# Attention followed by a sticky mixture of experts: a new order of the vector engine's round, other places for the operand splits and for the routing steps

## The chip, the cores and the metric

The kernel runs on one core of a Trainium2 chip. The metric is the device time of one execution in microseconds (us), as the median of the runs shown. Engines are named as in the profile: PE multiplies matrices (PEld loads their stationary side), DVE is the vector engine, ACT the scalar engine, POOL the GpSimd engine, and SP issues most of the DMA transfers.

## The reference

Two stages follow each other. The attention keeps, for each query, the first 4 keys and a window of 128 keys. The experts' stage picks for each token the expert with the largest logit, or keeps the expert of the token before it when a local gate says so, which makes the choice a scan along the sequence.

```python
# attention: batch 4, 8 heads, 768 positions, 64 per head, float32
scores = scale * np.matmul(q, k.transpose(0, 1, 3, 2))
keep = is_sink | in_window
scores = np.where(keep, scores, -1000000000.0)
a = np.exp(scores - np.max(scores, axis=-1, keepdims=True))
a = a / (np.sum(a, axis=-1, keepdims=True) + 1e-09)
x = np.matmul(a, v)                       # then reshaped to (4, 768, 512)
# experts: 8 of them, 512 -> 1024 -> 512
for s in range(S):
    fresh_e = int(np.argmax(logits[b, s]))
    e = fresh_e if s == 0 or local_gate[b, s] < 0.5 or prev_e < 0 else prev_e
    prev_e = e
    p = softmax(logits[b, s])
    out[b, s] = p[e] * (np.maximum(x[b, s] @ w1[e], 0.0) @ w2[e])
```

## The kernel before, in words

**Blocks, groups and rounds.** The attention works on 8 groups (4 batches by 2 halves of the heads, 4 heads each). A group has 6 blocks of 128 queries, numbered 0 to 5, so there are 48 blocks. The loop `for n in range(nb + 3)` runs rounds: round n scores block n, turns the probabilities of block n-1, multiplies block n-2 by the values and finishes block n-3. Rounds 0 to 47 have scores, rounds 48 to 50 drain the pipeline. PE, DVE and ACT run in the order in which this loop writes their instructions (`tc.manual_schedule`); POOL and SP get their order from the framework's planner. Every engine runs its own queue in order.

**One round.** `score` (L513) makes the scores of two units of two heads each. `out` runs once per unit: a DVE instruction masks the scores and takes their minimum (L525, two per unit), and ACT takes the exponential and its sum (L527). `pack` (L532, DVE) copies the sinks' probabilities of block n-1, where that block is 2 or later; PE turns them (L553), ACT copies them (L559) and DVE subtracts (L563). `turn` (L542, PE) and `turned` (L549, ACT) turn the other probabilities. `apply` (L573, L578, PE) multiplies by the values, `collect` (L466, DVE) copies the result out of PSUM, `back` (L470, PE) turns it back and multiplies by the gate weights, and `finish` (L485, L489, DVE) scales by the inverse sums. `sums` (L476, DVE) adds 1e-9 to the sums of the exponentials and `invert` (L479) inverts them.

Before the change DVE's order in a round is: out of unit 0, pack, out of unit 1, sums, finish, the subtraction L563, invert, one or more routing steps, collect.

**The splits.** Queries and keys are split into a high and a low part for a more exact product. For the next group POOL does this in `qk_split`: four copies (L118) and four subtractions (L123). `HEADS` says in which unit of the present group they are written; POOL waits only for its data and may run ahead of that place. Two tiles take turns: `w_a` for even groups, `qk_b` for odd ones.

**The routing.** When the last block of a batch is finished, `routing` is started as a generator, and `step` runs one piece of it, up to the next `yield`. Its pieces are: logits and their maximum (L238, L241); the choice (L247 to L261) and the exponentials' argument (L266); a transposition on PE (L274) with two ACT copies (L276, L278); two half scans (L286); two half counts (L293) with a rank (L295, on POOL for the first two batches, else on DVE); a matmul that brings slots and one-hot rows back (L301); slots and gates (L305 to L315); and six indirect stores per batch from POOL's queue into the buffer `xs` (L318). The fourth batch is routed in two parts: its first three blocks at the end of the attention, its last three (the tail) during the first expert rows. One step is taken per round before round 38, two from 38 on, three from 47 on.

**The first expert weights.** During the last group, `first_load` and `first_split` bring the first expert's first matrix and split it (L396 on DVE and ACT by turns, L397 on POOL, the last one on DVE). After round 50, `early_prep` turns the first rows of the first expert (L360) and the experts' stage begins: `ffn1` (L946, L955) and `second` (L1004).

Of the kernel before, what the change touches and what calls it, by code (L numbers as in the profile page):

```python
# [19 lines left out]
P = 128  # L20
# [25 lines left out]
FSK, FAST0 = 4, 38  # L46
LOADS = {0: (2,), 3: (0,), 4: (3, 1), 6: (4,), 8: (5,)}
HEADS = (6, 7, 9, 10), (4, 6, 8, 9)
LATER = 5, 6, 7, 8
# [3 lines left out]
RAW = 7200  # L53
WX = P + 2 * NW
# [10 lines left out]
def kernel(ctx, tc, qkd, vn, vs, w1, w2, nw, c_misc, c_ident, c_idw, c_small,  # L65
# [51 lines left out]
    def copy(e, out, in_):  # L117
        (nc.scalar.copy if e == "act" else getattr(nc, e).tensor_copy)(out, in_)  # L118

    lows = {}  # L120
# [4 lines left out]
    def qk_split(gi, eng, ahead=True, qc=slice(0, S), kc=slice(0, KPAD)):  # L125
        def part(p, x, cs, eng):
            hi, lo = qk_t[gi % 2][p][2 * x:2 * x + 2]
            r = raw[(gi * NPR + p) % NR][:, x]
            copy(eng[0], hi[:, cs], r[:, cs])
            low(eng[1], lo[:, cs], r[:, cs], hi[:, cs])  # L130
# [33 lines left out]
    with tc.tile_pool(name="ps_w", bufs=1, space=PS) as ps_w:  # L164
        wt = ps_w.tile([P, 512], F32, name="wt")
        zb = zrow.bitcast(BF16)
        for _ in range(WARM):
            nc.tensor.matmul(wt, zb[:, 0:P], zb[:, 0:512], start=True, stop=True)

# [42 lines left out]
    fk_t = rt.tile([P, NBLK, 40], BF16, name="fk")  # L212
    nc.gpsimd.memset(fk_t, 0.0)
# [17 lines left out]
    def routing(b, i0, i1, sfx, ps, ptag, apart=False):  # L231
# [4 lines left out]
        lg = rt.tile([P, NBLK, NW], F32, tag="lg", name=f"lg{n}")  # L236
        lg = lg[:, 0:nb]
        nc.vector.tensor_reduce(out=lg, in_=lw[:, i0:i1].rearrange("p i h e -> p i e h"), axis=AX.X, op=ALU.add)  # L238
        mx = rt.tile([P, NBLK], F32, tag="mx", name=f"mx{n}")
        mx = mx[:, 0:nb]  # L240
        nc.vector.tensor_reduce(out=mx, in_=lg[:, :, 0:E], axis=AX.X, op=ALU.max)  # L241
        if apart:
            yield
        mxb = mx.unsqueeze(2).broadcast_to([P, nb, E])
        eq = rt.tile([P, NBLK, E], F32, tag="eq", name=f"eq{n}")
        eq = eq[:, 0:nb]
        nc.vector.tensor_tensor(out=eq, in0=lg[:, :, 0:E], in1=mxb, op=ALU.is_equal)  # L247
        nc.vector.tensor_tensor(out=eq, in0=eq, in1=rank_w[:, 0:nb], op=ALU.mult)
        m2 = rt.tile([P, NBLK], F32, tag="m2", name=f"m2{n}")
        m2 = m2[:, 0:nb]  # L250
        nc.vector.tensor_reduce(out=m2, in_=eq, axis=AX.X, op=ALU.max)
        fr = rt.tile([P, NBLK], F32, tag="fr", name=f"fr{n}")
        fr = fr[:, 0:nb]

        nc.vector.scalar_tensor_tensor(out=fr, in0=lg[:, :, E], scalar=-1.5 * 2.0 ** -23,
                                       in1=first[:, i0:i1], op0=ALU.is_lt, op1=ALU.max)
        fk = fk_t[:, 0:nb]
        nc.vector.tensor_tensor(out=eq, in0=eq, in1=m2.unsqueeze(2).broadcast_to([P, nb, E]), op=ALU.is_equal)
        frb = fr.unsqueeze(2).broadcast_to([P, nb, E])
        nc.vector.tensor_tensor(out=fk[:, :, 0:E], in0=eq, in1=frb, op=ALU.mult)  # L260
        nc.vector.tensor_scalar(fk[:, :, 32:40], frb, -1.0, 1.0, op0=ALU.mult, op1=ALU.add)  # L261
        ex = rt.tile([P, NBLK, E], F32, tag="ex", name=f"ex{n}")
        ex = ex[:, 0:nb]
# [5 lines left out]
        if apart:  # L269
            chances()  # L270
            yield
        tf = ps.tile([40, S], BF16, tag=ptag, name=f"tf{n}")
        for j in range(nb):
            nc.tensor.transpose(tf[:, j * P:(j + 1) * P], fk[:, j, :], identb)  # L274
        fo = rt.tile([E, S], BF16, tag="fo", name=f"fo{n}")
        nc.scalar.copy(fo[:, 0:nq], tf[0:E, 0:nq])  # L276
        kp = rt.tile([E, S], BF16, tag="kp", name=f"kp{n}")
        nc.scalar.copy(kp[:, 0:nq], tf[32:32 + E, 0:nq])  # L278
        if not apart:
            chances()  # L280
        yield
        oh = orr.bitcast(F32)[0:E]
        cuts = [slice(c, c + nq // 2) for c in (0, nq // 2)] if apart and nb == NBLK else [slice(0, nq)]
        for c in cuts:
            s = q0 + c.start
            nc.vector.tensor_tensor_scan(orr[0:E, s:q0 + c.stop], kp[:, c], fo[:, c],  # L286
                                         0.0 if s == 0 else oh[:, s - 1:s], ALU.mult, ALU.add)
            yield
        ct = rt.tile([E, S], F32, tag="ct", name=f"ct{n}")
        rank_e = nc.gpsimd if b < B - 2 else nc.vector  # L290
        for c in cuts:
            o = oh[:, q0 + c.start:q0 + c.stop]
            nc.vector.tensor_tensor_scan(ct[:, c], ones8.broadcast_to([E, c.stop - c.start]), o,  # L293
                                         ct[:, c.start - 1:c.start] if c.start else run, ALU.mult, ALU.add)
            rank_e.tensor_tensor(out=orr[32:40, q0 + c.start:q0 + c.stop], in0=ct[:, c], in1=o, op=ALU.mult)  # L295
            if c.stop == nq:
                nc.vector.tensor_copy(run, ct[:, nq - 1:nq])
            yield
        tm = ps.tile([P, NBLK, 10], F32, tag=ptag, name=f"tm{n}")
        for j in range(nb):  # L300
            nc.tensor.matmul(tm[:, j, :], orr[:, q0 + j * P:q0 + (j + 1) * P], base_r, start=True, stop=True)  # L301
        if apart:
            yield
        slot = rt.tile([P, NBLK], I32, tag="slot", bufs=2, name=f"slot{n}")
        nc.vector.tensor_copy(slot[:, 0:nb], tm[:, 0:nb, 8])  # L305
        sm = rt.tile([P, NBLK], F32, tag="sm", name=f"sm{n}")
        sm = sm[:, 0:nb]
        nc.vector.tensor_reduce(out=sm, in_=ex, axis=AX.X, op=ALU.add)
        nc.vector.tensor_scalar(sm, sm, 1e-9, None, op0=ALU.add)
        nc.vector.reciprocal(sm, sm)  # L310
        nc.vector.tensor_tensor(out=ex, in0=tm[:, 0:nb, 0:E], in1=ex, op=ALU.mult)
        pp = rt.tile([P, NBLK], F32, tag="pp", name=f"pp{n}")
        pp = pp[:, 0:nb]
# [90 lines left out]
    def first_load():  # L404
        for c, t in enumerate(first_raw):
            nc.sync.dma_start(t, w1[0, c // 2 * P:(c // 2 + 1) * P, c % 2 * HP:(c % 2 + 1) * HP])
# [10 lines left out]
    def first_split(c):  # L417
# [834 lines left out]
```

## Time and profile before

| What | Value |
|---|---|
| median of 3 runs | 641.96 us (640.58 to 642.2) |
| profiled execution | 644.77 us, its span 643.0 us |
| PE busy | 548.6 us, 85% of the span |
| DVE busy | 376.9 us, 59% |
| ACT busy | 282.7 us, 44% |
| POOL busy | 237.2 us, 37% |
| first scores / first matmul of the experts | 6.57 us / 281.63 us |
| mean granted PE clock | 0.904 |

Rows of the timeline have the start in us from the span's start, the length in us, engine, line, operation, output and inputs, form and count; behind them, in brackets, how long the engine had been idle and what released it. Rows of merged instructions give the time from the first one's start to the last one's end. Rows of the table by windows give the window and its length, then the busy time of each engine with its count, the granted PE clock (1.00 is full), the DMA engines' share and GB/s.

### The profile page before, as it was taken

The numbers are of one execution on the slowest core, as the hardware profiler recorded it, in microseconds if no ns is written. First come the engines' busy times: TensorE is split into PE (matmuls) and PEld (weight loads), VectorE is DVE, ScalarE is ACT, GpSimd is POOL, SyncE is SP. The second block draws the span as 40 slices with busy tenths as digits, with TensorE's granted clock in tenths as the row PEclk, the third lists the DMA queues.
The fourth block names the chain that finished last, engine by engine and source line by source line (L and its number), as shares of the span: only waits on it lengthen the run. The fifth ranks groups of instructions, "written<-read, shape, count | busy, mean of one in ns | idle before, by whom it ended". The sixth has DMA issues, their size and how long they took to land. (4 is left out here: it accounts for less than half of the span.)

```text
span 643.0 us, 11713 instructions
## 1 busy us (share of the span) xinstructions
PE 548.6 (85%) x3872; PEld 468.9 (73%) x3872; DVE 376.9 (59%) x1255; ACT 282.7 (44%) x844; POOL 237.2 (37%) x191
## 2 busy tenths in 40 slices
PE   6799888778777776666958999998999979999995
PEld 3588776667656665556757997897798849897994
DVE  5778786589757467435463762838276395452521
ACT  3588855575637356022132631725063254321310
POOL 4875261836371053013151610625161264311301
PEclk8799978898978788657957999999999999999998
DMA  8622403241324032012923702756381365501000
GB/s 310 242 95 91 159 20 139 105 154 63 110 88 144 0 133 67 2 54 72 336 93 91 286 35 72 267 174 228 118 296 52 124 221 171 217 35 54 20 33 33
DMA packets 30475, 80.40 MB, mean 125 GB/s; under 512 B 3774, under 2 KB 5310, under 8 KB 30272
## 3 DMA queue, kind: packets, MB, share of 16 engines
q1 hardware_dynamic: 25520, 65.41, 29.3%
q0 software_dynamic: 4176, 12.64, 5.2%
q14 instruction: 149, 1.22, 0.6%
q8 instruction: 54, 0.88, 0.6%
q10 hardware_dynamic: 576, 0.25, 0.1%
HBM read 63.27 MB, written 16.06 MB: 123 GB/s over the span
## 5 line engine op out<-in xcount | busy, mean ns | idle before, releaser
L527 ACT ACTIVATE pef<-smf,biasf 128x264 f32<-128x264 f32 (+2 forms) x192 | 93.5, 489 | 73.6 <-DVE biasf L525 69.3
L525 DVE CUSTOM_DVE_ANT_0 smf<-sf,mask 128x264 f32<-128x264 f32 (+2 forms) x192 | 68.9, 400 | 16.3 <-PE sf L513 8.6
L966 ACT ACTIVATE hx<-h 128x256 fp32r<-128x256 f32 (+3 forms) x72 | 24.2, 359 | 106.8 <-PE h L955 92.2
L1004 PE MATMUL late<-w_a,hx 128*128 128x512 f32 (+2 forms) x288 | 68.8, 393 | 1.4 <-issue 1.4
L934 DVE SCALAR_TENSOR_TENSOR hx<-h,hx 128x256 fp32r<-128x256 f32 (+3 forms) x72 | 26.7, 391 | 68.5 <-ACT hx L966 64.5
L1004 PEld LDWEIGHTS late<-w_a,hx 128*128 128x128 f32 (+2 forms) x288 | 50.7, 179 | 14.8 <-issue 1.8
L578 PE MATMUL avf<-ptf,v 128*64 128x128 f32 x704 | 60.3, 323 | 0.0
L542 PE MATMUL tpf<-ident,pef 128*128 128x128 f32 x352 | 55.2, 299 | 5.3 <-ACT ptf L549 5.1
L1004 PE MATMUL late<-w_b,hx 128*128 128x512 f32 (+1 forms) x216 | 55.0, 412 | 2.4 <-SPq L879 2.1
L986 POOL DMA_INDIRECT out_dram<-ot_d,oi_d x18 | 18.7, 1040 | 103.0 <-DVE ot_d L985 82.0
L549 ACT COPY ptf<-tpf 128x512 f32<-128x512 f32 (+1 forms) x96 | 51.0, 532 | 10.7 <-PE avf L578 4.7
L1004 PEld LDWEIGHTS late<-w_b,hx 128*128 128x128 f32 (+1 forms) x216 | 41.5, 195 | 13.4 <-issue 2.3
L542 PEld LDWEIGHTS tpf<-ident,pef 128*128 128x128 f32 x352 | 40.9, 150 | 14.1 <-ACT ptf L549 6.9
L578 PEld LDWEIGHTS avf<-ptf,v 128*64 128x64 f32 x704 | 46.9, 162 | 5.0 <-issue 0.6
L966 ACT ACTIVATE hx<-hs 128x96 fp32r<-128x96 f32 (+2 forms) x72 | 16.7, 273 | 72.5 <-DVE hs L949 65.5
L318 POOL DMA_INDIRECT xs<-xb,slotf x21 | 20.5, 978 | 68.8 <-DVE early_i L338 32.8
L470 PE MATMUL bkf<-idw,xtf 128*128 128x146 f32 x192 | 37.0, 320 | 5.6 <-DVE xtf L466 5.4
L835 POOL TENSOR_TENSOR w_b<-raw,w_b 128x1024 fp32r<-128x1024 f32 x10 | 25.1, 2511 | 44.6 <-ACT w_b L834 37.0
L835 POOL TENSOR_TENSOR w_c<-raw,w_c 128x1024 fp32r<-128x1024 f32 x11 | 27.8, 2528 | 33.2 <-ACT w_c L834 27.8
L485 DVE TENSOR_TENSOR xb<-bkf,zf 128x256 f32<-128x256 f32 x48 | 20.2, 421 | 30.5 <-ACT ptsf L559 26.2
L835 POOL TENSOR_TENSOR w_a<-raw,w_a 128x1024 fp32r<-128x1024 f32 x10 | 26.5, 2651 | 29.8 <-ACT w_a L834 22.8
L527 ACT ACTIVATION_READ_ACCUMULATOR pef<-smf,biasf 128x1 f32 x192 | 36.2, 189 | 0.0
(232 smaller groups left out, 1163.9 us busy)
## 6 DMA issues: line engine op xcount, KB each, us to landing
raw<-in_dram SPq DMA_DIRECT2D x53, 512.0 KB, 5.3
raw<-in_dram SPq DMA_DIRECT2D x14, 800.0 KB, 7.0
xr_0n<-xs SPq DMA_DIRECT2D x21, 258.0 KB, 4.0
v<-in_dram SPq DMA_DIRECT2D x7, 768.0 KB
raw_w<-in_dram SPq DMA_DIRECT2D x7, 512.0 KB, 4.9
raw<-in_dram SPq DMA_DIRECT2D x10, 256.0 KB, 5.1
xs<-zrun SPq DMA_DIRECT2D x9, 258.0 KB, 4.7
xr_0r<-xs SPq DMA_DIRECT2D x8, 258.0 KB, 3.3
```

The lines of the kernel that those rows point to most:

```text
L318: s_i = nc.gpsimd.indirect_dma_start(out=xs[:, :], out_offset=bass.IndirectOffsetOnAxis(ap=slot[:, j:j + 1].bitcast(U32), axis=0), in_=xb[ ...
L470: mm = nc.tensor.matmul(bk[:, pr * WX:(pr + 1) * WX], blk["xt"][:, pr, :], idw[:, g * NPR + pr, :], start=True, stop=True, skip_group_chec ...
L485: nc.vector.tensor_tensor(out=xb[:, i, g * HG * D:(g + 1) * HG * D].rearrange("p (r t d) -> p r t d", r=NPR, t=2), in0=av[:, :, 0:P].rearr ...
L525: nc.vector.tensor_tensor_reduce(out=sm[:, :w], in0=sps[:, t, :w], in1=mk, scale=-0.125, scalar=BIG, op0=ALU.add, op1=ALU.min, accum_out=b ...
L527: nc.scalar.activation(pe[:, h, :w], sm[:, :w], AF.Exp, bias=bias[:, t:t + 1], scale=-1.0, accum_out=z[:, h:h + 1])
L542: nc.tensor.transpose(tp[:, t, k, :], pe[:, 2 * c + t, o:o + P], ident)
L549: nc.scalar.copy(pt[:, :, 0:nt, :], tp[:, :, 0:nt, :])
L578: nc.tensor.matmul(avt[ROWS[t], pr, :], prep["v"][:, j, 2 * pr + t, :], x["pt"][:, t, k, :], start=i < 2 and pr == 0 and k == 0, stop=pr = ...
L835: todo += [lambda s=s: lo(out=l[:, s], in0=raw[:, s], in1=h.bitcast(F32)[:, s], op=ALU.subtract) for s in ([slice(0, FF)] if eng[1] == "po ...
L934: nc.vector.scalar_tensor_tensor(out=d[:, :, 1, :], in0=h, scalar=0.0, in1=d.bitcast(F32)[:, :, 0, :], op0=ALU.max, op1=ALU.subtract)
L966: relu = nc.scalar.activation(d[:, :, 0, :], h, AF.Relu)
L1004: nc.tensor.matmul(o, a, w, start=t == 0, stop=t == len(mm) - 1, skip_group_check=half)
```

## The change: what it does

- **Order.** Pack and collect move to the front of DVE's round, ahead of both units' out. The routing steps come behind `apply` in PE's queue; before they came ahead of it.
- **Sums.** The sums live in a tile `sum_z` with four places, beside constants 1e-9; `sums` becomes a tensor_reduce over the pair.
- **Splits.** `HEADS` writes the splits of queries and keys in block 0 of a group, and the first copy waits for a DVE instruction of that block's first unit (`behind`).
- **Steps.** `STEPS` and `ENDING` say how many routing steps a round takes: before the last group (rounds 42 to 47) none in blocks 0 and 1 of a group, one or two in the later ones; in the last group one or two in most rounds. The pieces are cut anew: logits; maximum and choice; final choice, exponentials and half the transposition; the other half with the first scan; the second scan with the first count; the second count with the matmul and an ACT copy of its result; slots; stores.
- **Transposition.** In halves, with one ACT copy each; the two rows of choice and stay have 8 columns each and no padding.
- **First weights.** ACT makes all eight high parts in blocks 2 to 5 of the last group, POOL all low parts one round later; the loads start a group earlier.
- **The tail.** Its first piece ends before the transposition; the others follow.

```diff
-FSK, FAST0 = 4, 38
+STEPS = {2: 1, 3: 1, 4: 1, 5: 1, 9: 1, 10: 1, 11: 2}
+ENDING = {38: 1, 39: 1, 40: 1, 41: 1, 42: 1, 43: 1, 44: 2, 45: 1, 47: 1, 48: 2, 49: 2, 50: 2}
-HEADS = (6, 7, 9, 10), (4, 6, 8, 9)
+HEADS = {6: (0,), 7: (1,), 9: (2,), 10: (3,)}, {0: (0, 1), 1: (2, 3)}
...
+            i = copy(eng[0], hi[:, cs], r[:, cs])
+            if behind:
+                tc.add_manual_dep(i.ins, behind.pop().ins.name, ...)
...
+sum_z = at.tile([P, NZ, HG, 2], F32, name="sum_z")
+nc.gpsimd.memset(sum_z, 1e-9)
...
             def sums(blk):
-                nc.vector.tensor_scalar(blk["z"], blk["z"], 1e-9, None, op0=ALU.add)
+                nc.vector.tensor_reduce(out=rs, in_=blk["z"], axis=AX.X, op=ALU.add)
...
+        def turn(h):
+            tf = ps.tile([E, 2, hb * P], BF16, tag=ptag, name=f"tf{n}_{h}")
+            for j in parts[h]:
+                for a in range(2):
+                    nc.tensor.transpose(tf[:, a, (j - h * hb) * P:(j - h * hb + 1) * P], fk[:, j, a], identb)
+            nc.scalar.copy(kf[:, h, :, 0:w], tf[:, :, 0:w])
+
+        def stay(h):
+            nc.vector.tensor_tensor_scan(orr[0:E, s:s + w], kf[:, h, 1, 0:w], kf[:, h, 0, 0:w], ...)
+
+        def count(h):
+            nc.vector.tensor_tensor_scan(ct[:, c:c + w], ones8.broadcast_to([E, w]), o, ...)
+            rank_e.tensor_tensor(out=orr[32:40, q0 + c:q0 + c + w], in0=ct[:, c:c + w], in1=o, op=ALU.mult)
...
         if apart:
             chances()
+        turn(0)
+        if apart:
             yield
+        for h in range(1, len(parts)):
+            turn(h)
+            stay(h - 1)
+            if apart:
+                yield
...
+        for h in range(len(parts)):
+            if apart and h == len(parts) - 1:
+                yield
+            count(h)
...
         if apart:
+            tp, tm = tm, tile("tms", 10)
+            nc.scalar.copy(tm, tp)
             yield
...
+                    if deep:
+                        pack(a[0]["blk"], nm)
+                    if y:
+                        collect(y[0]["blk"], nm)
                     if now:
                         out(now[0])
-                    if deep:
-                        pack(a[0]["blk"], nm)
...
-                    for _ in range(1 if n < FAST0 else 2 if n < nb - 1 else 3):
-                        step()
                     if z:
                         apply(z, nm)
-                        collect(z[0]["blk"], nm)
+                    weights(n, now[0] if now else None)
+                    for _ in range((ENDING if n >= nb - 2 * NBLK + 2 else STEPS).get(...)):
+                        step()
```

174 lines of the change are left out of this document (91 added, 83 removed).

## The prediction

> **What bounds the kernel now.** I read the page first, then the table by windows.
>
> ```profile
> PE 548.6 (85%) x3872; PEld 468.9 (73%) x3872; DVE 376.9 (59%) x1255; ACT 282.7 (44%) x844; POOL 237.2 (37%) x191
> 37.09:58.19 21.10, 21.10 (x242) 18.53 (x241) 17.56 (x87) 18.15 (x65) 11.69 (x11) 1.00 0.32 122
> 65.03:127.06 62.03, 51.62 (x496) 43.67 (x494) 44.92 (x194) 38.76 (x134) 28.86 (x28) 0.89 0.29 108
> 127.06:191.47 64.41, 50.11 (x494) 42.21 (x492) 49.78 (x194) 38.09 (x131) 33.75 (x31) 0.92 0.30 103
> 191.47:246.65 55.18, 43.29 (x372) 36.43 (x370) 35.89 (x161) 30.19 (x99) 14.01 (x15) 0.81 0.27 92
> 246.65:281.63 34.98, 18.65 (x120) 15.62 (x118) 17.74 (x68) 8.57 (x24) 6.68 (x6) 0.64 0.11 40
> 345.00:643.00 298.00, 280.44 (x1643) 243.16 (x1641) 147.82 (x345) 105.99 (x267) 94.02 (x53) 0.99 0.39 134
> ```
>
> The reader is to see five stretches. A group without routing (37.09 to 58.19, rounds 6 to 11) takes 21.10 us and PE is busy in all of it. Two groups are 42.2 us; rounds 14 to 25, with batch 0's routing, take 62.0, rounds 26 to 37 take 64.4. Rounds 38 to 46, one and a half groups (31.7 quiet), take 55.2. The last round, the drain and the start of the experts take 35.0 with 18.7 of PE. Behind 345 PE is full, and no edit reaches it. So the change can work on about 90 us, of which PE's own work at full clock needs less than half.
>
> What lengthens a round is read from one quiet round (round 10), in order of time:
>
> ```profile
> 51.42 0.42 DVE L525 CUSTOM_DVE_ANT_0 smf<-sf,mask 128x264 f32<-128x264 f32 x1
> 51.94 0.52 ACT L527 ACTIVATE pef<-smf,biasf 128x264 f32<-128x264 f32 x1 [0.50 <-DVE biasf L525]
> 52.12 0.25 DVE L532 COPY pkf<-pef 128x96 f32<-128x96 f32 x1
> 52.28 0.42 DVE L525 CUSTOM_DVE_ANT_0 smf<-sf,mask 128x264 f32<-128x264 f32 x1
> 53.42 0.26 ACT L559 CAST ptsf<-bkf 96x128 fp32r<-96x128 f32 x1
> 53.71 0.42 DVE L485 TENSOR_TENSOR xb<-bkf,zf 128x256 f32<-128x256 f32 x1 [0.56 <-ACT ptsf L559]
> 54.79 0.42 DVE L466 COPY xtf<-avf 128x256 f32<-128x256 f32 x1
> 55.13 0.42 DVE L525 CUSTOM_DVE_ANT_0 smf<-sf,mask 128x264 f32<-128x264 f32 x1
> ```
>
> DVE's out starts ACT's exponentials, ACT reaches the sinks' copy L559, finish waits for that copy, and finish, invert, step and collect stand ahead of the next out. This ring takes 55.13 - 51.42 = 3.71 us, as long as PE's round. Whatever DVE does between finish and the next out, a step above all, is therefore added whole to the round; pack at 52.12 lies beside the 0.56 us wait and is free.
>
> **The port.** Some DVE instructions take as long as POOL's split beside them:
>
> ```profile
> 82.67 2.33 DVE L286 TENSOR_TENSOR_SCAN orr<-kpf,fof 8x384 fp32r<-8x384 bf16 x1
> 88.87 0.97 DVE L286 TENSOR_TENSOR_SCAN orr<-kpf,orr,fof 8x384 fp32r<-8x384 bf16 x1
> 93.60 2.74 DVE L293 TENSOR_TENSOR_SCAN ctf<-ones,zrun,orr 8x384 f32<-8x384 f32 x1
> 93.64 1.90 POOL L123 TENSOR_TENSOR w_a<-raw,w_a 128x800 fp32r<-128x800 f32 x1
> 182.86 3.70 DVE L476 TENSOR_SCALAR zf<-zf 128x4 f32<-128x4 f32 x1
> 182.88 3.65 POOL L123 TENSOR_TENSOR qk_b<-raw,qk_b 128x768 fp32r<-128x768 f32 x2
> L476 DVE TENSOR_SCALAR zf<-zf x48: 152/166/3704, 15.1 to 258.6; 128x4 f32<-128x4 f32 x48
> L238 DVE TENSOR_REDUCE lgf<-lw x4: 519/945/981, 68.2 to 253.1; 128x54 f32<-128x432 f32 x3, 128x27 f32<-128x216 f32 x1
> ```
>
> A half scan takes 0.97 us, 2.33 or 2.74 beside POOL; L476 takes 0.17 at the median and once 3.70. The reduction L238 never leaves its range.
>
> **The change part by part.** *Sums and scans off the port.* The scans lost 2.33 + 2.74 - 2 x 0.97 = 3.1 us in batch 0 (batch 1 has the like), all on the ring; the new steps put them where POOL should be done. A late sum stands on the ring only where it outlasts the wait at finish, chiefly the 3.70 (3.5 us over the median). The reduction that replaces it works on 4 pairs: I take L241's 0.21 us, 0.04 over the old median, and it stands ahead of the 0.56 us wait, so it costs nothing; without that cover 48 x 0.04 = 1.9 us. The Trainium skill, page "VectorE: DVE Perf Modes", section "Rules for kernel authors", calls tensor_reduce the slowest DVE op and advises against it on a hot path; by that rule this edit would cost the 1.9 us.
>
> *Pack to the front.* It leaves the free place and enters the ring: 52.28 - 52.12 = 0.16 us in four rounds of six, 1.3 per batch. In block 3 it must also wait for ACT's last exponential of the round before; I take 0.5 us per group where no step lies there. If ACT were earlier, nothing; at most a whole exponential, 0.52.
>
> *Steps.* Their DVE work stays, now without the port:
>
> ```profile
> 194.59 0.98 DVE L238 TENSOR_REDUCE lgf<-lw 128x54 f32<-128x432 f32 x1
> 195.61 0.21 DVE L241 TENSOR_REDUCE mxf<-lgf 128x6 f32<-128x48 f32 x1
> 196.57 0.21 DVE L258 TENSOR_TENSOR eqf<-eqf,m2f 128x48 f32<-128x48 f32 x1
> 197.15 0.41 DVE L466 COPY xtf<-avf 128x256 f32<-128x256 f32 x1
> 110.77 0.16 DVE L305 CAST slotf<-tmf 128x6 int32<-128x6 f32 x1
> 111.91 0.42 DVE L466 COPY xtf<-avf 128x256 f32<-128x256 f32 x1
> 99.64 0.99 POOL L295 TENSOR_TENSOR orr<-ctf,orr 8x384 fp32r<-8x384 f32 x1 [2.17 <-DVE ctf L293]
> 102.17 0.87 PE L301 MATMUL tmf<-base_r,orr 40*128 40x10 f32 x6 [0.30 <-ACT ptf L549]
> ```
>
> Logits 0.98, choice 0.96 (195.61 to 196.57), end of the choice 0.58 (to 197.15), four half scans and counts 4 x 0.97 plus a copy, slots 1.14: 7.7 us per batch. New are two waits of PE, because its work now stands in the same piece as what it needs, with the next scores queued behind: the half transposition behind the choice (round 16, I take 0.7 over the ring) and the matmul behind second count and rank (round 22: 0.97 + 0.99 + half of 0.87 after invert, then scores; about 2.1 over the ring). If DVE is early enough these two cost nothing; if POOL's rank is late by one subtraction, 1.9 us (93.64) more. The transposition has twelve small matmuls for six, about 0.5 us more of PE per batch, inside these waits. Gone is the tie of one of the two PSUM buffers until DVE reads the slots; ACT's copy of 60 columns frees it.
>
> *Splits.* Per quiet group POOL has 11.7 us (the windows' row), which from block 0's first out ends in block 3, and the next group needs them at its block 0: some 8 us to spare. Behind the waiting first copy POOL holds seven more splits and the sinks' copies of the next group; for them wait the next group's scores, and on SP the loads that reuse the raw tiles, with the values' loads behind them. None is due before the next group's first rounds. The six early weight loads on SP find their raw tiles free once group 6 is split. After a batch they queue behind six stores:
>
> ```profile
> 114.41 0.96 POOL L318 DMA_INDIRECT xs<-xb,slotf  x1 [0.30 <-issue]
> 122.29 0.42 DVE L485 TENSOR_TENSOR xb<-bkf,zf 128x256 f32<-128x256 f32 x1 [3.02 <-ACT ptsf L559]
> L295 DVE TENSOR_TENSOR orr<-ctf,orr x3: 547/547/548, 209.5 to 263.9; 8x384 fp32r<-8x384 f32 x3
> 289.99 2.51 DVE L295 TENSOR_TENSOR orr<-cts,orr 8x384 fp32r<-8x384 f32 x1
> 292.55 0.80 PE L301 MATMUL tms<-base_r,orr 40*128 40x10 f32 x3 [3.99 <-DVE orr L295]
> ```
>
> The stores take POOL 6 x 1.26 = 7.6 us, and around them all engines stand still at times (122.29: DVE 3.02 us, ACT's queue equally late): batch 0's stores cost about 4 us in rounds 24 to 26, and nothing in the change removes that; I keep 4, 4 and 3 us. Behind the stores the splits run until about block 4 of batch 1's and batch 2's first groups, while the choice (block 3) and what follows it read two SBUF tensors, as the rank does: 2.51 us at 289.99, beside POOL, for 0.55 elsewhere. I bound what the steps lose there: nothing if POOL is done, 8 us (all its subtractions of a group, 4 x 1.90 and a copy's rest) if they alternate with it, and take 2.5 for each of the two batches, since choice and POOL overlap by about that. The Trainium skill, page "SBUF — State Buffer", section "Who interferes with whom", says that a DVE instruction with two SBUF inputs contends with GpSimd's reads and the later one fully blocks, while tensor_reduce never contends on trn2. This rule speaks against these places for the steps and, taken in full, gives the rival Less; 289.99 and the steady L238 agree with it.
>
> *First weights.* ACT gets two more copies a round in rounds 44 to 47:
>
> ```profile
> 242.82 0.62 ACT L396 CAST w_a<-raw 128x512 fp32r<-128x512 f32 x1
> 255.00 0.51 PE L274 MATMUL tff<-identb,fk 128*40 128x128 bf16 x3 [5.54 <-DVE fk L261]
> 264.57 0.77 PE L301 MATMUL tmf<-base_r,orr 40*128 40x10 f32 x3 [4.04 <-DVE orr L295]
> 281.19 0.51 PE L274 MATMUL tfs<-identb,fk 128*40 128x128 bf16 x3 [5.54 <-DVE fk L261]
> ```
>
> In blocks 3 to 5 ACT's work (from 51.94 to the end of the next unit's exponentials and copies, about 3.5 us) plus 1.24 is longer than the ring by 0.8 a round. Loads come early enough, and POOL's low parts end in round 49.
>
> *Drain.* Before, apply of the last blocks stood in PE's queue behind the routing of the last half batch and waited with it (5.54, 4.04). Now it stands ahead, and the first step is taken in round 47. I write the new chain from round 47's first out, T (247.58 before), with the quiet round's steps (finish T+2.3, invert done T+3.4). Logits of three blocks (0.52, L238's row) T+3.9; ACT's weight copies end T+5.3, its copies for round 48 T+6.2, finish to invert T+7.3, choice T+8.6, half transposition and ACT's copy T+10.1. Round 49: collect T+9.1, back and finish T+10.7, scan T+11.7, count and rank T+13.3, matmul T+14.0. Round 50: collect T+13.9, finish T+15.4, slots T+16.7, early_prep's second subtraction T+18.3. From there to the tail's first instruction it was 2.2 us, so PE starts the experts at T+20.5; before it was T+34.0 (281.63). I take off 1 us for POOL's low parts beside the choice, and 0.5 for the late round 47, and book 12; bounds 8 (PE at half clock: back and apply twice as long) and 15. Two of the 12 come from the tail's first piece, which no longer holds PE (281.19).
>
> *Tail.* PE waited 3.99 us at 292.55 for a rank; its matmul is now two pieces later. The store is later too; I take 3 us, with 0 (the stores are what counts) and 4 as bounds.
>
> **The sum.** Each stretch is built anew from the quiet one (us; profiled execution 644.8, its span 643.0):
>
> - to round 13: one late sum less, pack more: 0;
> - rounds 14 to 25: 42.2 + 7.7 steps + 1.3 pack + 0.5 its wait + 2.8 PE's waits + 4 stores = 58.5 for 62.0: -3.5;
> - rounds 26 to 37: 58.5 + 2.5 port = 61.0 for 64.4: -3.4;
> - rounds 38 to 46: 31.7 + 7.7 + 2.1 (two ranks of 0.55 on DVE and the early counts, 1.0) + 1.0 pack + 1.0 PE's waits (one falls into a short block) + 1.6 ACT + 3 stores + 2.5 port = 50.6 for 55.2: -4.6;
> - drain -12, tail -3.
>
> Together -26.5: 618.3 for a profiled execution. The median of the runs shown, 641.96, lies 2.8 under the profiled one, so 615.5.
>
> **Rivals.**
> *More (593).* The steps never meet POOL (5), the stores disturb no longer (4 + 4 + 3), and PE's new waits hide (2.8 + 2.8 + 1.0): 22.6 more. For it: 37.09 to 58.19 shows that the engines can run at PE's pace. Against: a step lies in a ring without slack.
>
> *Less (628.5).* The new places miss their aim: POOL's order is the planner's, its splits start later than now, and choice and scans meet them in full (2 x 5.5 over my value) while the drain wins 2 less: 13 back. A split so late that the next group's scores wait needs 8 us more and is counted here.
>
> *Slower (651.5): PE's clock falls.* In the steps' rounds PE is busy for 3.5 us (21.10 / 6) of about 5, in pieces. At half clock that becomes 7.0 at most, 2 us over my round. From 14 of the 24 such rounds on the gain of 26.5 is gone; with 18 of them the time is 615.5 + 36 = 651.5. For it: 0.64 in the drain and 0.81 in rounds 38 to 46, where PE waited. Against: with 83% of PE (51.62 of 62.03) it kept 0.89, with 78% 0.92.
>
> **How the numbers follow.** Forecast 0.60, with its own range 603 to 627 (port 0 to 8 twice, drain 8 to 15, tail 0 to 4, stores each 0 to 5). More 0.17, Less 0.13, Slower 0.07, 0.03 for a change too small to tell, which is 0.3% (2 us) for this kernel. The range 594 to 634 takes in More and Less and leaves out the clock, no change and gains beyond 48. Faster is the sum of the first three, 0.90; same 0.03; slower 0.07.
>
> **What would show it.** Right: no sum above 0.3 us in rounds 6 to 50; scans at 0.97; pack, collect and out adjacent, the ring of a quiet round near 3.87; rounds with steps at 4.5 to 5.9, the one with second count and matmul near 7 with PE waiting there; first matmul of the experts some 20 us behind round 47's out. Wrong: a quiet group above 23 us, a choice blocked for more than 2.5 us in each of blocks 3, a clock below 0.8 in rounds 14 to 41, or scores that wait for POOL.

## The result and the profile after

The changed kernel takes 602.61 us (median of 4 runs, 600.66 to 605.69); the kernel before took 642.08 us beside it. The ratio is 0.9394, with a 95% interval of 0.9343 to 0.9444: 39 us less, where 26.5 were forecast. The profiled execution took 604.36 us, its span is 602.5 us. All ratios in this document leave out slower executions of a kernel (two of four of the run a_ahead, one of six of same2).

First the busy time of the engines, on the page of the changed kernel, then its table by windows (stretch; its length, then busy time and count of PE, PEld, DVE, ACT and POOL; PE's granted clock, DMA share, GB/s).

```profile
PE 533.5 (89%) x3896; PEld 454.6 (75%) x3896; DVE 356.8 (59%) x1250; ACT 285.0 (47%) x850; POOL 237.7 (39%) x192
```

```profile
6.05:62.40 56.35, 49.40 (x505) 41.69 (x505) 40.41 (x202) 41.07 (x146) 38.40 (x39) 0.88 0.50 192
...
33.91:55.27 21.36, 21.36 (x243) 18.53 (x242) 16.55 (x86) 17.77 (x65) 11.90 (x11) 1.00 0.31 120
62.40:118.25 55.85, 48.73 (x500) 41.85 (x499) 38.98 (x186) 37.84 (x130) 26.01 (x24) 0.94 0.30 114
118.25:176.54 58.29, 50.07 (x498) 41.73 (x498) 41.79 (x194) 37.92 (x131) 32.50 (x32) 0.94 0.34 116
176.54:225.31 48.77, 40.72 (x374) 33.91 (x374) 33.67 (x160) 32.19 (x108) 13.97 (x16) 0.90 0.25 88
225.31:245.34 20.03, 14.16 (x119) 11.67 (x118) 14.51 (x62) 10.76 (x30) 9.57 (x9) 0.83 0.26 82
245.34:280.10 34.76, 29.51 (x169) 25.06 (x170) 19.25 (x60) 9.27 (x21) 10.57 (x7) 0.90 0.56 194
```

Two more stretches of the kernel before, from the same view, are needed beside those that the prediction shows: from the first scores to round 14, and the tail.

```profile
6.57:65.03 58.46, 49.93 (x505) 42.21 (x504) 45.08 (x201) 41.30 (x147) 38.74 (x39) 0.88 0.48 182
...
281.63:320.22 38.59, 32.13 (x164) 28.03 (x164) 17.38 (x50) 9.72 (x22) 8.38 (x5) 0.80 0.45 160
```

The reader is to see that every stretch became shorter, with PE's clock higher in most. The tail is the start of the experts, up to 280.10 us (before 320.22). Stretch by stretch, the gain that was forecast and the gain that the traces show:

```
stretch                     before   after   gain   forecast
first scores                  6.57    6.05    0.5      -
rounds 0 to 13               58.46   56.35    2.1      0
rounds 14 to 25              62.03   55.85    6.2      3.5
rounds 26 to 37              64.41   58.29    6.1      3.4
rounds 38 to 46              55.18   48.77    6.4      4.6
round 47 to first expert     34.98   20.03   15.0     12
tail                         38.59   34.76    3.8      3
rest                        322.78  322.40    0.4      0
```

In the changed kernel a group without routing takes 21.36 us (before 21.10), all of it PE. Against it, rounds 14 to 25 are longer in six rounds only, by the starts of their scores: round 16 by 2.9 us, 17 by 1.9, 22 by 4.8, 23 by 1.7 (the steps), 24 and 25 by 1.8 together (the stores). Rounds 18 to 21 run at the quiet pace. Rounds 22 and 23 in order of time, cut to the rows that set them:

```profile
96.19 0.97 DVE L286 TENSOR_TENSOR_SCAN orr<-kff,orr 8x384 fp32r<-8x384 bf16 x1
97.09 0.98 DVE L292 TENSOR_TENSOR_SCAN ctf<-ones,zrun,orr 8x384 f32<-8x384 f32 x1
98.00 0.22 DVE L568 COPY pkf<-pef 128x96 f32<-128x96 f32 x1
...
98.25 0.42 DVE L500 COPY xtf<-avf 128x256 f32<-128x256 f32 x1
...
98.58 0.42 DVE L560 CUSTOM_DVE_ANT_0 smf<-sf,mask 128x264 f32<-128x264 f32 x1
...
101.85 0.97 DVE L292 TENSOR_TENSOR_SCAN ctf<-ones,ctf,orr 8x384 f32<-8x384 f32 x1
...
102.90 0.98 POOL L294 TENSOR_TENSOR orr<-ctf,orr 8x384 fp32r<-8x384 f32 x1 [3.76 <-DVE ctf L292]
...
103.94 0.27 PE L327 MATMUL tmf<-base_r,orr 40*128 40x10 f32 x1 [2.64 <-POOL orr L294]
103.95 0.39 PE L548 MATMUL sf<-qk_b 64*128 64x264 f32 x1
...
105.21 0.43 DVE L560 CUSTOM_DVE_ANT_0 smf<-sf,mask 128x264 f32<-128x264 f32 x1 [1.60 <-PE sf L548]
```

Scan, count, pack, collect and out follow each other on DVE without a gap, each at its undisturbed price. PE waits 2.64 us for the rank, the next scores (103.95) wait behind it, and the ring from out to out is 105.21 - 98.58 = 6.63 us (the prediction said near 7). From out to out rounds 15, 16, 17 and 21 take 4.8, 4.9, 5.9 and 5.7 us, as the prediction had it (4.5 to 5.9); round 14, with the logits, takes 3.7, near its quiet 3.6, and round 23 takes 6.1. Then PE's clock falls:

```profile
103.95:109.59 5.64, 5.64 (x47) 5.15 (x47) 2.34 (x12) 2.99 (x11) 4.17 (x4) 0.70 0.00 0
```

This is round 23: PE is busy in all of its 5.64 us, at a clock of 0.70; a quiet round there takes 3.93.

The sums and the half scans, from the views of their lines (duration: minimum, median, maximum in ns):

```profile
L511 DVE TENSOR_REDUCE rsf<-sum_z x48: 144/156/160, 15.0 to 232.0; 128x4 f32<-128x8 f32 x48
...
L286 DVE TENSOR_TENSOR_SCAN orr<-kff x4: 914/925/1656, 81.0 to 237.5; 8x384 fp32r<-8x384 bf16 x4
L286 DVE TENSOR_TENSOR_SCAN orr<-kff,orr x3: 974/975/975, 96.2 to 202.5; 8x384 fp32r<-8x384 bf16 x3
```

No sum leaves 0.16 us, and one scan of seven was blocked (1.66). In the traces of the runs same and same2, the same kernel again, two and one were (1.66 to 1.71). The end of the drain:

```profile
227.45 0.42 DVE L560 CUSTOM_DVE_ANT_0 smf<-sf,mask 128x264 f32<-128x264 f32 x1
...
230.95 0.51 DVE L248 TENSOR_REDUCE lgf<-lw 128x27 f32<-128x216 f32 x1
...
240.07 0.80 PE L327 MATMUL tmf<-base_r,orr 40*128 40x10 f32 x3 [1.44 <-DVE orr L294]
...
244.51 0.69 DVE L390 TENSOR_TENSOR x_a<-xpfe,x_a 128x512 fp32r<-128x512 f32 x1
...
245.34 3.06 PE L1000 MATMUL h_s<-x_a,w_a 128*128 128x256 f32 x24 [1.49 <-DVE x_a L390]
```

The experts start 17.9 us behind round 47's first out (245.34 - 227.45); before it was 34.05.

### The profile page after: what moved, and what is told of

Same layout as the page of the kernel before. It is cut to its first block, busy times and chain, and to the rows that moved or that the text cites. A ratio compares the mean times of both kernels' runs of the same rounds, so it can differ in the third digit from the quotient of the medians.

```text
span 602.5 us, 11755 instructions
## 1 busy us (share of the span) xinstructions
PE 533.5 (89%) x3896; PEld 454.6 (75%) x3896; DVE 356.8 (59%) x1250; ACT 285.0 (47%) x850; POOL 237.7 (39%) x192
## 3 DMA queue, kind: packets, MB, share of 16 engines
q1 hardware_dynamic: 25520, 65.41, 31.5%
## 5 line engine op out<-in xcount | busy, mean ns | idle before, releaser
L560 DVE CUSTOM_DVE_ANT_0 smf<-sf,mask 128x264 f32<-128x264 f32 (+2 forms) x192 | 66.8, 402 | 20.3 <-PE sf L548 9.9
L578 PE MATMUL tpf<-ident,pef 128*128 128x128 f32 x352 | 57.3, 306 | 1.9 <-ACT ptf L585 1.6
L614 PE MATMUL avf<-ptf,v 128*64 128x128 f32 x704 | 51.7, 287 | 1.5 <-issue 1.5
L1049 PEld LDWEIGHTS late<-w_b,hx 128*128 128x128 f32 (+1 forms) x216 | 40.8, 192 | 13.4 <-issue 2.6
L578 PEld LDWEIGHTS tpf<-ident,pef 128*128 128x128 f32 x352 | 42.1, 153 | 11.3 <-ACT ptf L585 4.4
L614 PEld LDWEIGHTS avf<-ptf,v 128*64 128x64 f32 x704 | 39.1, 140 | 7.1 <-issue 2.8
L520 DVE TENSOR_TENSOR xb<-bkf,rsf 128x256 f32<-128x256 f32 x48 | 20.3, 423 | 36.2 <-ACT ptsf L595 28.0
L548 PE MATMUL sf<-w_a 64*128 64x264 f32 (+2 forms) x288 | 28.8, 320 | 10.8 <-POOL w_a L125 3.4
L880 POOL TENSOR_TENSOR w_a<-raw,w_a 128x1024 fp32r<-128x1024 f32 x10 | 26.5, 2649 | 27.0 <-ACT w_a L879 24.9
```

What stands on the lines that cost most here:

```text
L548: u["mm"] = nc.tensor.matmul(sps[:, t, :w], qx[ROWS[t], i * P:(i + 1) * P], kx[ROWS[t], off:off + w], start=m == 0, stop=m == 2)
L560: u["dve"] = nc.vector.tensor_tensor_reduce(out=sm[:, :w], in0=sps[:, t, :w], in1=mk, scale=-0.125, scalar=BIG, op0=ALU.add, op1=ALU.min, ...
L578: nc.tensor.transpose(tp[:, t, k, :], pe[:, 2 * c + t, o:o + P], ident)
L614: nc.tensor.matmul(avt[ROWS[t], pr, :], prep["v"][:, j, 2 * pr + t, :], x["pt"][:, t, k, :], start=i < 2 and pr == 0 and k == 0, stop=pr = ...
L880: todo += [lambda s=s: lo(out=l[:, s], in0=raw[:, s], in1=h.bitcast(F32)[:, s], op=ALU.subtract) for s in ([slice(0, FF)] if eng[1] == "po ...
L1049: nc.tensor.matmul(o, a, w, start=t == 0, stop=t == len(mm) - 1, skip_group_check=half)
```

## The experiments

The runs were made on three chips, those of one group on the same chip with the kernel before beside them. On two of the chips the kernel before took 632.2 and 631.2 us, on the third 642.8, as in the result. So ratios are compared inside a group; where the first group needs the changed kernel, the 0.9501 of the last group (same2) is taken, from a chip on which the kernel before took the same time. Of the kernel before there is one trace, the result's.

```
run       edit                                   before    ratio   95% interval
a_sums    after, sums by tensor_scalar            632.2   0.9566  0.9493 to 0.9639
a_heads   after, splits in the old places         632.2   0.9444  0.9377 to 0.9512
a_order   after, old order of pack and collect    632.2   0.9446  0.9371 to 0.9521
a_ahead   after, pieces ahead of apply            632.2   0.9837  0.9731 to 0.9942
same      the changed kernel                      642.8   0.9399  0.9328 to 0.9470
b_apply   before, apply ahead of the pieces       642.8   0.9767  0.9711 to 0.9824
a_fill    after, PE filled where it waited        642.8   0.9334  0.9277 to 0.9391
a_late    after, pieces cut later                 642.8   0.9349  0.9295 to 0.9402
same2     the changed kernel                      631.2   0.9501  0.9454 to 0.9548
late2     after, pieces cut later and moved       631.2   0.9386  0.9340 to 0.9432
late3     late2, old order of pack and collect    631.2   0.9401  0.9364 to 0.9437
b_sums    before, sums by tensor_reduce           631.2   0.9918  0.9885 to 0.9951
```

### The sums alone, both ways

```diff
-                nc.vector.tensor_reduce(out=rs, in_=blk["z"], axis=AX.X, op=ALU.add)
+                nc.vector.tensor_scalar(blk["z"], blk["z"], 1e-9, None, op0=ALU.add)
```

This is a_sums (with the sums in a tile of their own, as before). b_sums is the reverse edit in the kernel before.

> The changed kernel, with the sums by tensor_scalar on a tile of their own again; all else as changed. Theory 1 (the port): the subtractions now run in blocks 0 to 2, so the sums of those blocks stand beside them; one blocked for up to 1.8 us outlasts the 0.7 us wait at finish by about 1 us in two or three rounds of each of seven groups and at the early weights: 14 us more, 612 to 622, with sums of 1 to 2 us in the trace. Theory 2 (the extra gain is PE's clock, the sum's time is hidden in blocks that PE bounds): at most 4 us more, 602 to 607, and no quiet group longer than 22.5 us.

> The kernel before with one edit: the sums by tensor_reduce over a second, constant column, as in the change. Theory 1 (blocked sums outlast the wait at finish and are added to the ring; undoing this edit cost 3 us by round 14): 4 to 9 us less than before, ratio 0.986 to 0.994, 2 to 3 us of it by round 14. Rival (the blocked sums stand in rounds that PE bounds): less than 2 us, above 0.997.

b_sums takes 0.8% (5 us) off the kernel before, as theory 1 said; but up to round 14 its trace is only 0.8 us shorter than that of the kernel before (57.67 for 58.46 us, on another chip), where 2 to 3 were expected. a_sums is 0.65% (4 us) above the changed kernel and not the 14 us of theory 1; the intervals overlap. In the trace of a_sums the sums are blocked again; first their line, then one of them beside POOL:

```profile
L510 DVE TENSOR_SCALAR zf<-zf x48: 163/214/4190, 15.5 to 228.8; 128x4 f32<-128x4 f32 x48
```

```profile
121.06 1.83 POOL L125 TENSOR_TENSOR qk_b<-raw,qk_b 128x768 fp32r<-128x768 f32 x1
121.36 4.19 DVE L510 TENSOR_SCALAR zf<-zf 128x4 f32<-128x4 f32 x1
...
122.83 0.85 POOL L120 CAST qk_b<-raw 128x800 fp32r<-128x800 f32 x1
...
123.65 1.86 POOL L125 TENSOR_TENSOR qk_b<-raw,qk_b 128x800 fp32r<-128x800 f32 x1
```

A sum of 0.16 us lasts until POOL has done a subtraction, a copy and another subtraction. But half of the sums take 0.214 us or less, and a quiet group is only 0.8 us longer, 22.16 us for 21.36. The mechanism holds; its price in a quiet group was put too high by the expectation.

### The places of the splits

```diff
-HEADS = {6: (0,), 7: (1,), 9: (2,), 10: (3,)}, {0: (0, 1), 1: (2, 3)}
+HEADS = {6: (0,), 7: (1,), 9: (2,), 10: (3,)}, {4: (0,), 6: (1,), 8: (2,), 9: (3,)}
...
-                        if gi and not h:
-                            behind.append(u["dve"])
```

> The changed kernel, with the q/k splits of groups 1 to 6 in the places of before (blocks 2 to 4, no wait behind the out). Theory 1: choice, scans and POOL's rank meet the subtractions again; 3 us of blocked scans and choice and 2 to 4 us of late rank in each of two batches: 8 to 14 us more, 611 to 617, scans of 2 us or more in rounds 15 to 23 and 27 to 35. Rival: with sums on tensor_reduce the place of the splits hardly counts: 602 to 606.

The ratio is 0.9444 for 0.9501, so theory 1 fell: with the sums on tensor_reduce, the old places are no slower. A half scan was blocked once in each of two batches (2.49 and 2.46 us):

```profile
L286 DVE TENSOR_TENSOR_SCAN orr<-kff x4: 915/1694/2494, 80.2 to 229.3; 8x384 fp32r<-8x384 bf16 x4
```

The other scans stayed at 0.98 us in the old places as well.

### The order of pack and collect

```diff
+                    if now:
+                        out(now[0])
                     if deep:
                         pack(a[0]["blk"], nm)
-                    if y:
-                        collect(y[0]["blk"], nm)
-                    if now:
-                        out(now[0])
```

with collect behind the pieces at the end of the round (a_order in the changed kernel, late3 in late2, below).

> The changed kernel, with pack between the two outs and collect at the end of the round again. Theory 1: both orders put the same instructions on DVE's ring, and PE sets the pace of a quiet round: 600 to 606, the same within 0.5%. The prediction's own terms (pack 1.3 us and its wait 0.5 us per group pair come back): 597 to 600. Rival (sinks' transposition and back come earlier, and the extra gain is this): 608 to 615, and a quiet group longer than 22 us.

> late2, and pack between the two outs, collect at the end of the round, as before the change. Theory 1 (pack and its wait for ACT lie on the ring of the rounds with steps, 1.8 us for each batch by the prediction and 1.9 us in rounds 14 to 25 of a_order): another 3 to 6 us less than late2. Rival (the order is worth nothing here; a_order was within the interval of the result): within 2 us of late2.

In both cases the intervals overlap with that of the kernel that was cut. In a_order's trace rounds 14 to 25 take 52.93 us. That is 1.9 less than a_heads's 54.86 on this chip, but a_heads has other places for the splits; the changed kernel itself takes 54.03 in the trace of same2, 1.1 more than a_order. The prediction gave 1.8 to pack and its wait; the whole time does not show it. For late3 theory 1 fell: the order is worth nothing that can be measured.

### Apply and the pieces on PE's queue

a_ahead is the changed kernel with the loop that takes the routing's pieces moved ahead of apply, as it stood before. b_apply is the kernel before with this edit alone:

```diff
-                    for _ in range(1 if n < FAST0 else 2 if n < nb - 1 else 3):
-                        step()
                     if z:
                         apply(z, nm)
+                    for _ in range(1 if n < FAST0 else 2 if n < nb - 1 else 3):
+                        step()
+                    if z:
                         collect(z[0]["blk"], nm)
```

> The changed kernel, with the routing's pieces ahead of apply in each round, as before the change. Theory 1: where PE waits in a piece, apply (1.5 us) now stands behind the wait: 1.5 us in two rounds of each of three batches, and about 4 us in the drain: 10 to 15 us more, 612 to 618. Rival (the drain was shortened by its earlier start alone, the order inside a round is hidden): 602 to 606, with the first expert matmul still 18 us behind round 47's first out.

> The kernel before, with one edit: apply stands ahead of the routing's pieces on PE instead of behind them; collection stays at the end of the round. Theory 1 (the order on PE's queue is the largest single part of the gain, since a_ahead lost 28 us by it): 10 to 20 us less than before, ratio 0.970 to 0.985, granted clock above 0.91. Rival (in the kernel before a round lies between DVE's part and PE's part of a step, so that apply waits only in the drain): 3 to 6 us less, 0.990 to 0.995, the drain alone shorter.

b_apply takes 15.0 us off the kernel before (theory 1 said 10 to 20): the largest single part of the gain that was found. a_ahead gives back 3.4%, some 21 us, more than either theory said. Where b_apply won it, first in the kernel before, then in b_apply (rounds 14 to 46 in one row):

```profile
65.03:246.65 181.62, 145.02 (x1356) 122.31 (x1354) 130.59 (x549) 107.04 (x364) 76.62 (x72) 0.88 0.28 102
```

```profile
64.90:235.89 170.99, 135.94 (x1354) 113.48 (x1352) 130.55 (x549) 106.64 (x364) 76.55 (x72) 0.93 0.30 108
```

DVE's and ACT's busy time is the same; PE needs 9 us less for the same matmuls, since it runs at 0.93 of its clock and not 0.88: busy time times clock is nearly the same, 145.02 x 0.88 = 127.6 and 135.94 x 0.93 = 126.4. In round 18 of each, the kernel before and then b_apply:

```profile
86.18 0.42 PE L553 MATMUL bkf<-ident,pkf 128*96 128x128 f32 x1 [1.95 <-DVE pkf L532]
...
87.82 1.98 PE L578 MATMUL avf<-ptf,v 128*64 128x128 f32 x16
```

```profile
85.45 0.29 PE L553 MATMUL bkf<-ident,pkf 128*96 128x128 f32 x1 [1.35 <-DVE pkf L532]
...
86.33 1.09 PE L578 MATMUL avf<-ptf,v 128*64 128x128 f32 x16
```

PE's wait differs by 0.6 us (the half scan ahead of pack was blocked to 2.33 us in the one and to 1.75 in the other, so that the order is not its only cause), and behind the longer one apply takes 1.98 us for 1.09; the round takes 7.40 us in the one and 5.17 in the other. The drain became shorter by 4.9 us (34.98 to 30.07), a third of what the whole change wins there.

### PE filled where it waits

```diff
                         apply(z, nm)
+                        for _ in range(FILL.get(n, 0)):
+                            nc.tensor.matmul(z[0]["blk"]["spare"], zrow.bitcast(BF16)[:, 0:P],
+                                             zrow.bitcast(BF16)[:, 0:NPR * P], start=True, stop=True, ...)
```

The tile of apply is twice as large, and its second half is the spare one. FILL gives 12 matmuls in rounds 16, 28, 40 and 22 in rounds 22, 34, 43.

> The changed kernel itself, so that the other runs of this call have it beside them on the same chip. Every theory: its ratio to before is that of the result, 0.934 to 0.944; in the trace, the stretches of rounds 14 to 25, 26 to 37 and 38 to 46 within 2 us of 55.9, 58.3 and 48.8, or shorter where the stores of a batch disturb less than in that trace.

> The changed kernel; in rounds 16, 28, 40 twelve and in rounds 22, 34, 43 twenty-two matmuls of zeros (128 x 256, bf16) stand behind apply, into a half of its bank that nobody reads, so that PE works where it waited for choice and rank. Nothing is left out. Theory 1 (the half clock in rounds 17, 23, 35 and 44 follows PE's standing still, and costs 1.5 to 2.5 us each time): 4 to 8 us less than the changed kernel, clock 1.00 in those rounds. Rival (the clock does not hang on these waits): within 2 us of the changed kernel, or up to 4 us more where the fill outlasts the wait, with the same dips.

Rounds 22 and 23 of the changed kernel on this chip, then of a_fill:

```profile
94.02:102.80 8.78, 4.93 (x49) 3.82 (x47) 7.44 (x25) 4.71 (x17) 1.98 (x2) 0.93 0.14 52
102.80:109.45 6.65, 6.65 (x46) 6.13 (x46) 2.43 (x13) 3.12 (x12) 4.16 (x4) 0.58 0.00 0
```

```profile
93.75:102.52 8.77, 7.39 (x71) 5.88 (x69) 7.44 (x25) 4.70 (x17) 1.97 (x2) 1.00 0.14 55
102.52:106.60 4.08, 4.08 (x48) 3.69 (x48) 2.32 (x12) 2.76 (x10) 3.09 (x4) 1.00 0.02 4
```

Round 22 is as long as without the fill (8.77), and round 23 is 2.6 us shorter at full clock; so it is in the next batch (round 35: 6.67 us without the fill, 4.08 with it). That is theory 1: the half clock behind the wait comes from PE's standing still. The whole is 4 us less (0.9334 for 0.9399), though the intervals overlap: in the third batch round 43 grew from 6.86 to 9.79 us.

### Pieces cut so that PE does not wait

a_late joins choice and end of the choice, puts both half transpositions into one piece and adds a yield ahead of the matmul by rank; the last line of the diff is late2's, whose last pieces come a round earlier:

```diff
-        if not apart:
+        if not apart or nb == NBLK:
             yield
         tm = ps.tile([P, NBLK, 10], F32, tag=ptag, name=f"tm{n}")[:, 0:nb]
...
-STEPS = {2: 1, 3: 1, 4: 1, 5: 1, 9: 1, 10: 1, 11: 2}
+STEPS = {2: 1, 3: 1, 4: 1, 5: 1, 8: 1, 9: 1, 10: 1, 11: 2}
```

> The changed kernel, with the pieces cut so that PE finds its data ready: the end of the choice goes with the choice (round 15), both half transpositions come in round 16, the first half scan alone in 17, the matmul by rank stands in round 23 ahead of the slots instead of in 22; the same for the next two whole batches. Theory 1 (PE's waits and the half clock behind them are what the steps cost beyond DVE's time): 1 us less at the transposition and 3.5 us less at the matmul in each of three batches, 9 to 14 us less than the changed kernel. Rival (the wait only changes its engine: DVE waits for ACT's copy of the slots, and the ring sets the round): 0 to 3 us less.

> The changed kernel itself again, beside the next three on one chip. Every theory: ratio to before 0.934 to 0.944.

> The changed kernel with the pieces of a_late, and besides the last pieces one round earlier: second half scan and first count in block 2 of the next group, second count in 3, the matmul by rank in 4, slots and stores in 5 (in the third batch rounds 42 to 45). In a_late the slots, moved to where POOL splits, were blocked for 1.6 us and waited for ACT's copy. Theory 1 (what the steps must cost is DVE's own time alone, 3.9 us in these rounds, for 6.5 us in the changed kernel): 2 to 3 us less in each of three batches, 6 to 9 us less than the changed kernel. Rival (PE's wait only turns into another wait on DVE's ring, as in a_late): 0 to 3 us less.

a_late gains 3 us only (0.9349 for 0.9399), as its rival said. PE's wait is gone, and DVE has got one:

```profile
106.99 0.20 ACT L334 COPY tmsf<-tmf 128x60 f32<-128x60 f32 x1
...
107.23 1.62 DVE L337 CAST slotf<-tmsf 128x6 int32<-128x6 f32 x1 [0.52 <-ACT tmsf L334]
```

The slots wait for ACT's copy, and the cast of 128 x 6 numbers, read from SBUF beside POOL's subtractions, takes 1.62 us for 0.14. late2, which brings the slots ahead of the splits, is 1.2% faster than the changed kernel beside it (0.9386 for 0.9501, medians 592.98 and 601.52 us; theory 1 said 6 to 9 us) and beats both kernels. In its trace rounds 22, 23 and 24 take 14.24 us at full clock, for 18.16 in the trace of the changed kernel:

```profile
95.71:101.38 5.67, 4.83 (x49) 3.76 (x47) 4.37 (x18) 3.94 (x15) 0.99 (x1) 1.00 0.12 38
101.38:105.45 4.07, 4.07 (x48) 3.68 (x47) 3.25 (x17) 3.46 (x15) 3.12 (x4) 1.00 0.00 0
105.45:109.95 4.50, 4.08 (x45) 3.37 (x43) 3.41 (x22) 2.66 (x11) 3.02 (x3) 1.00 0.13 50
```

## Why the prediction was right, and where its sum was off

The direction holds, and so does the order of the stretches by size: 26.5 us were forecast, 39 measured. The time, 602.6 us, lies just below the forecast's own range (603 to 627) and inside the wider one (594 to 634). The mechanism holds in part. The chain of the drain, PE's waits in it and the blocked sums were seen rightly. In rounds 14 to 46 PE's clock behind its waits, by b_apply the largest cause, stood in no term; where a sum came out near there (54.5 us for 54.0 in rounds 14 to 25, without the stores), that was partly luck. Each miss has its term.

**To round 13 (0 forecast, 2.1 measured).** The late sums were set off against pack. b_sums shows them: its round 4 takes 3.81 us, that of the kernel before 5.67. Pack costs 0.26 us in a quiet group. What else came off in rounds 2 and 3 (1.2 us) stays open.

**Steps, pack and PE's waits.** For rounds 14 to 25 the sum had 54.5 us without the stores; the trace has 42.7 + 11.3 = 54.0. This is right in size, though two errors cancel in it: the logits and most of pack cost nothing, since PE sets the length of those rounds (round 15 has its quiet 3.59 us), and PE's waits cost more than their 2.8 us, because the clock fell behind them, which was in no term. In the two later batches the steps cost 9.2 and 9.3 us, 2 to 3 less than forecast: rounds 29 and 41 (4.2 us) had no half clock, where round 17 (5.8 us) had.

**The port (2.5 twice).** In the result's trace this term is empty: no choice was blocked (of what follows it, one cast of the slots was, 1.16 us for 0.14). It is not wrong as a mechanism. late2, on another chip, has it as the prediction put it, the choice in round 27 beside a subtraction that came late because it stood behind the stores:

```profile
121.46 0.20 POOL L407 COPY xb<-small 128x6 int32<-128x6 int32 x1 [1.45 <-DMA xs<-xb,slotf]
...
121.66 1.86 POOL L125 TENSOR_TENSOR qk_b<-raw,qk_b 128x800 fp32r<-128x800 f32 x1
...
121.89 1.65 DVE L258 SCALAR_TENSOR_TENSOR frf<-lgf,small 128x6 f32<-128x6 f32 x1
...
123.70 0.68 DVE L265 TENSOR_TENSOR fk<-eqf,frf 128x48 bf16<-128x48 f32 x1
```

That is 1.5 + 0.5 us over the undisturbed durations (0.15 and 0.21). The changed kernel itself on that chip (the trace of same2) has it in both batches: one instruction of the choice takes 1.60 us for 0.15 in round 27, two take 1.90 and 0.76 for 0.21 each in round 39, and rounds 28 and 40, which wait for the choice, take 8.57 and 9.36 us, where round 16 takes 6.87. In the result's trace DVE came to the choice later, held up by the stores' standstill in round 26, and POOL was done. So the sum added two terms of which, in these traces, one excludes the other.

**Stores (4, 4 and 3 us, and 1.6 for ACT in rounds 45 and 46).** The rounds behind the stores are longer by 1.8 + 3.6 (rounds 24 to 26), 2.2 + 4.2 (36 to 38) and 3.3 us (45 and 46): 15 for 12.6, two thirds of batch 0's and of batch 1's one stretch later than put. On the chip of late2 and same2 rounds 25 and 26 take 3.35 and 3.04 us in the one and 3.30 and 3.04 in the other, the quiet lengths but for 0.16: there the stores lengthen no round that follows them by more. That the gain was 31.5 us on that chip (0.9501, where 0.934 to 0.944 was expected) and 39 on the other is mostly the time of the kernel before, which differs by 10.9 us, while the changed kernel's differs by 1.1 (medians). On that chip the changed kernel spares the disturbance of the stores, but pays for the port.

**Drain (12; 15.0 measured).** The chain was right to within 1 us at each step: logits forecast to end at T+3.9, measured T+4.0; matmul by rank T+14.0 and T+13.4; early_prep's second subtraction T+18.3 and T+17.8. The step that failed is the last, "2.2 us" from there to the experts: they start 0.1 us behind it. Round 47's first out came later behind its scores (1.2 us for the 0.5 booked), and the 1 us for POOL's low parts did not come.

**Tail (3; 3.8 measured).** PE's wait for the rank of the tail is 1.65 us, for 3.99 before, which is 2.3 of the 3.8.

```profile
256.37 0.49 PE L327 MATMUL tms<-base_r,orr 40*128 40x10 f32 x3 [1.65 <-DVE orr L294]
```

**What the forecast gave to the wrong edit.** It put the order of apply and pieces into the drain alone. b_apply shows that it was worth 15 us, two thirds of it in rounds 14 to 46, by PE's clock; the sums off the port 5 us; the new places of the splits (and with them of the scans) and of pack and collect nothing measurable. If the parts add, 11 us remain of the 31.5 on the one chip and 19 of the 39 on the other (finer pieces, the earlier first step of the last half batch, the first weights); they were not taken apart, so this part of the gain has no cause shown.

**What the change can work on.** The prediction says about 90 us; by its own rows the five stretches stand 19.8 + 22.2 + 23.5 us over their quiet lengths, and 35.0 us from round 47 on come to it: 100. No term rests on this.

**The rivals.** Less needed choice and scans to meet POOL in full; late2 and same2 show part of it. Slower, PE's clock, had the right mechanism with the wrong sign: the new waits do halve the clock in rounds 17, 23, 35 and 44, but the old ones did so for longer (0.88 over rounds 14 to 46, after the change 0.94, 0.94 and 0.90).

## What to carry to other kernels

On an in-order engine, put work that is ready ahead of an instruction that must wait, and cut a step so that the waiting instruction stands a round behind what it needs. On TensorE a wait of 1.6 to 2.6 us can cost more than itself: the next 3 to 7 us may run at half clock, so look at the granted clock of the round behind a wait before pricing it. After removing one wait look for the next on the ring: here it went from PE to DVE, by way of a tiny cast from SBUF beside GpSimd, and only moving the slots as well made the gain.

## What the runs showed of the hardware

**The same gap, with and without the half clock.** Round 16 to 17 in two executions of the changed kernel, the result's and that of the run same: PE stands still for 1.6 us, works, and is then at half clock in one and at full clock in the other.

```profile
73.80:75.42 1.62, 0.00 (x0) 0.00 (x0) 1.34 (x8) 1.62 (x6) 0.00 (x0) 1.00 0.00 0
...
77.25:80.45 3.20, 3.20 (x18) 3.07 (x18) 1.27 (x9) 2.11 (x8) 3.20 (x4) 0.50 0.00 0
```

```profile
73.73:75.34 1.61, 0.00 (x0) 0.00 (x0) 1.33 (x8) 1.61 (x6) 0.00 (x0) 1.00 0.00 0
...
77.20:80.40 3.20, 3.20 (x42) 2.84 (x41) 2.40 (x12) 3.20 (x12) 3.20 (x4) 1.00 0.00 0
```

The Trainium skill, page "TensorE: Matmul & The Clock Gate", section "What's actually happening", says that the clock is set by a window of about 3.4 us that runs freely and does not start with the work, and that it falls after an idle window. The free-running window agrees with these two executions; that the fall needs some 3.4 us without work does not, since a gap of 1.62 us, followed by 1.77 us of work, stood ahead of the half clock here.

**Tiny operations are blocked as long as large ones.** tensor_scalar on 128 x 4 took up to 4.19 us, a cast of 128 x 6 1.62, a scalar_tensor_tensor of 128 x 6 1.65, each beside POOL's subtraction; tensor_reduce never left 0.144 to 0.160 us in 48 sums. The Trainium skill, page "VectorE: DVE Perf Modes", section "Rules for kernel authors", calls tensor_reduce the slowest DVE operation. For four pairs it took 0.156 us at the median, and the tensor_scalar before it 0.166, so the 1.9 us that the rule would have cost did not come. The Trainium skill, page "SBUF — State Buffer", section "Who interferes with whom", lets tensor_scalar contend with GpSimd and never tensor_reduce on trn2. Both halves of this agree with the durations above.

**Chips differ in what the stores disturb.** Where the kernel before took 631 or 632 us, rounds 25 and 26 kept their length within 0.2 us behind six stores (same2 and late2, and a_heads and a_order on the chip of the first group); where it took 642, they grew by 1.7 and 3.6 us in the result's trace and by 1.2 and 2.6 in that of same, with PE, DVE and ACT standing still at times. What in the chip does this was not found.
